# RWKV-7 recurrence followed by a squared-ReLU FFN: TensorE's work from chunk 4 on is grouped by how the array is divided, with FFN groups of two chunks

## The chip, the cores and the metric

The kernel runs on one core of one Trainium2 chip. The metric is the device time of one execution in microseconds (us). TensorE is called PE in the profile, VectorE DVE, ScalarE ACT, GpSimd POOL and SyncE SP; PEld is TensorE's weight load.

## The reference

Inputs `r, k, v, w, a, b` are float32 of 4 batches, 8 heads, 768 steps, 40 dimensions. The FFN's weights come as float64 (320 x 2048 and 2048 x 320). The output is float32, 3072 x 320.

```python
state = np.zeros((B, H, D, D))
for t in range(S):
    y[:, :, t] = np.einsum('bhd,bhde->bhe', rt, state)
    Sa = np.einsum('bhde,bhe->bhd', state, at)
    state_decay = state * wt[:, :, None, :] - np.einsum('bhd,bhe->bhde', Sa, bt)
    state = state_decay + np.einsum('bhd,bhe->bhde', vt, kt)
x = y.transpose(0, 2, 1, 3).reshape(B * S, H * D)
h = np.maximum(x @ w_in, 0.0)
out = (h * h) @ w_out
```

## The kernel before

The 768 steps are cut into 6 chunks of 128 steps for each of 4 batches. The 24 chunks (batch and place) are numbered in the order in which they run, the four batches in turn, so a chunk needs the state that the chunk four earlier left. All matmuls are float32; the trace shows each as two instructions, a transpose as one.

One chunk passes through four pieces of code, each a Python generator whose `yield` marks a place where other work may be put in between:

- `early` (called by `prepare`) turns `w`, `b`, `a` on PE, makes the running products of the decay and their reciprocals on DVE (`decay`), and makes on PE the 128 x 128 matrix N of each head (`products(bT, aT)`, L87), which goes to DRAM (`kept_d`, `kept_n`). It runs up to nine chunks ahead and ends with chunk 23 in slot 14.
- `solving` inverts the triangular halves of N on POOL (L443, L445: `half_p`, `half_t`) in units of 1 to 4 chunks and writes the inverse T to DRAM (`kept_t`). From chunk 4 on the units are chunks 4 to 5, 6 to 7, 8 to 9, 10 to 13, 14 to 17, 18 to 21 and 22 to 23. `inverses` reads T back (L459) on SP's queue.
- `rest` turns `k`, `r`, `v` and the decay on PE, makes the masked products A (k with a) and RV (v with r), decays the state, scales `k` and `b`, and turns the state (`sd`). It runs one chunk ahead.
- `chain` is the serial part: xw = v.A + state.a (L575 on); transposed (L588); times T (`times_t`, 64 x 64 quadrants); times N; times T again; transposed (L617); the new state (`grown`, from k, v and b, xn); the masked product RX; y = state.r + RV.k + RX.b. Between two steps ACT copies the result from PSUM to SBUF. y times the decay goes to `tokens`.

The main loop has a slot for each chunk i: `chain(i)`, `rest(i + 1)`, one or two `prepare`s and a share of the FFN are woven by `weave` in 12 steps by their numbers of pieces. Each engine runs its instructions in the order in which this Python code emits them.

The FFN (`ffn`, L664) works in groups of `GB = 3` chunks (384 tokens). The first layer's 320 inputs are 2 full tiles of 128 rows (`w_in`) and a rest of 64 rows (`w_third`). Two output tiles f share a step: two matmuls of 64 rows, in the array's two row halves, then four of 128 rows, then a ReLU on ACT for each (L679), then a square on DVE (L661). The second layer takes a chunk of 128 tokens at a time, 16 matmuls of 320 columns in four pieces. `by_then` sets how many pieces are done by the end of each slot: none before slot 4, 40 of 160 by the end of slot 9, 137 by the end of slot 23, the other 23 after the last slot.

PSUM is three pools of 128 x 512 banks: `ps_w` (4), `ps_c` (2, the chain's), `ps_f` (2, the FFN's). A bank is taken in turn, and its next user waits until the last reader is done.

How PE is divided follows from the operands: a matmul with 64 (or 40) rows uses half the rows (`64*128`; the profile writes `40*128`), one with a 64-wide result half the columns (`128*64`), one with both a quadrant (`64*64`), all others the whole array (`128*128`). In what follows a change of division between one PE instruction and the next is called a switch.

Of the kernel before, what the change touches and what calls it, by code (L numbers as in the profile page):

```python
# [11 lines left out]
Alu = mybir.AluOpType  # L12
# [5 lines left out]
def kernel(  # L18
# [34 lines left out]
    GB = 3  # L53
# [146 lines left out]
    hidden = single("hid", [128, NF, GB * C])  # L200
    free_words = hidden.rearrange("p f t -> p (f t)")
# [135 lines left out]
    def spare(name, i):  # L337
        at = NF * GB * C - (("mv", "turned", "joins").index(name) * 2 + i % 2 + 1) * H * Q
        return free_words[:, at:at + H * Q].rearrange("p (h t) -> p h t", h=H)

    def early(i, g=None):
# [12 lines left out]
        bT_, aT_ = turn(x_["b"]), turn(x_["a"])  # L354
        nc.vector.reciprocal(down[:, :, MID + 1:C + 1], up[:, :, MID + 1:C + 1])  # L355
        nc.vector.reciprocal(up[:, :, :MID], down[:, :, :MID])  # L356
        yield
        bT = turned("bT", 1)
# [142 lines left out]

    def rest(i, g):
        bb, c = order[i]
        x_ = loaded.pop(i)
        dec = g["dec"]
        up, down, aT = dec[:, UP], dec[:, DOWN], dec[:, A_, :, :C]
        ends = new("ends", [128, NP], 2)
        g["up"], g["aT"] = up, aT
        yield

        kT, rT = turned("kvT", 1), turned("rT", 2)
        kT_ = turn(x_["k"])
        yield
        nc.vector.tensor_tensor(kT, kT_, down[:, :, 1:C + 1], Alu.mult)  # L514
        nc.vector.tensor_copy(ends, down[:, :, 0])
        joining = inverses(i, g) if i else iter(())
        if soon(i):
            next(joining, None)
        yield
        g["A"] = masked("A", 2, kT, aT)  # L520
        yield
        while "v" not in x_:
            line.pop(0)[1]()
        nc.scalar.copy(rT, turn(x_["r"]))  # L524
        vT = turned("kvT", 1)
        nc.scalar.copy(vT, turn(x_["v"]))
        g["rT"] = rT
        yield
        if c > 0:
            st = states.tiles[bb]  # L530
            f_ = new("f", [128, NP], 1)
            nc.vector.tensor_tensor(f_, ended[bb], ends, Alu.mult)
            for e in range(2):
                own_ = st[e * DP:(e + 1) * DP, :, e, :D]
                nc.vector.tensor_tensor(own_, own_, f_[e * DP:(e + 1) * DP].unsqueeze(2).to_broadcast([DP, NP, D]), Alu.mult)
        g["RV"] = masked("RV", 4, vT, rT)
        if i and unit_of[i] < FINE:
            next(joining)
        yield
        p_ = psum(ps_w)  # L540
        for q in range(NP):
            nc.tensor.transpose(p_[:, q * 128:(q + 1) * 128], down[:, q, 1:C + 1], ident)  # L542
        inv = p_.rearrange("t (h d) -> t h d", h=H)[:, :, :D]
        yield
        for nm in ("k", "b"):
            nc.vector.tensor_tensor(x_[nm][:, :, :D], inv, x_[nm][:, :, :D], Alu.mult)
            g[nm] = x_[nm]
        g["v"] = x_["v"]
        if c > 0:
            p_ = psum(ps_c)  # L550
            for q in range(NP):
                nc.tensor.transpose(p_[:, q * 128:(q + 1) * 128], st[:, q].rearrange("p e d -> p (e d)"), ident)
            sd = g["sd"] = new("sd", [128, NP, 2, DP], 2)
            nc.scalar.copy(sd.rearrange("p q e d -> p q (e d)"), quads(p_))
        yield
        yield from joining
        yield
# [6 lines left out]
    def swap(t_, e):  # L564

        t_ = t_.rearrange("p (f t) -> p f t", f=2)
        return t_[:, ::-1] if e else t_

    def chain(i, g):
        bb, c = order[i]  # L570
        st = states.tiles[bb]
        aT, rT, k_, b_, v_ = (g[x] for x in ("aT", "rT", "k", "b", "v"))
        sd = g.get("sd")
        first, second_ = slice(0, HC), slice(HC, C)

        xw = quads(psum(ps_c))
        for h, q, e, rows in heads:
            mm(swap(xw[rows, q], 0), v_[:, h, :], swap(g["A"][e][:, q], e), h < 2)
        if c > 0:
            for h, q, e, rows in heads:  # L580
                mm(swap(xw[rows, q], 0), st[rows, q, e, :], swap(aT[rows, q], e), False)
        xc = turned("xnT", 1)
        nc.scalar.copy(xc, xw)
# [36 lines left out]
        yield  # L620
        if c < NCH - 1:
            grown = psum(ps_c)[:, :NP * D].rearrange("p (q d) -> p q d", q=NP)
            for l_, r_ in ((k_, v_), (b_, xn)):
                for h, q, e, rows in heads:
                    mm(grown[rows, q], l_[:, h, :], r_[:, h, :D], l_ is k_ and h < 2)
            for e in range(2):
                rows = slice(e * DP, (e + 1) * DP)
                nc.vector.tensor_tensor(st[rows, :, e, :D], grown[rows], st[rows, :, e, :D], Alu.add)
            ended[bb] = new(f"end{bb}", [128, NP], 1)
            nc.vector.tensor_copy(ended[bb], g["up"][:, :, C])  # L630
            yield
# [4 lines left out]
        if c > 0:  # L636
            for q in range(NP):
                mm(y_[:, q], sd[:, q].rearrange("p e d -> p (e d)"), rT[:, q], q == 0)
        for m_, rows in ((g["RV"], k_), (rx, b_)):
# [17 lines left out]
    PART = NF // 4  # L657

    def square(tiles):
        for h_ in tiles:  # L660
            nc.vector.tensor_tensor(h_, h_, h_, Alu.mult)  # L661

    def ffn():
        for gi in range(len(order) // GB):  # L664
            while gi not in gathered or finished[0] < NARROW:
                yield False
            t_ = tokens.pop(gi)
            hid = []
# [209 lines left out]
```

## Time and profile before

| | us |
|---|---|
| median of 3 runs (lowest, highest) | 1050.5 (1047.3, 1051.26) |
| profiled execution, first to last instruction | 1045.6 |
| PE busy | 927.4 (89%) |
| POOL busy | 670.6 (64%) |
| DVE busy | 496.8 (48%) |
| ACT busy | 273.0 (26%) |
| `tokens` of chunk 3, 9, 14, 23 begin at | 230.8, 470.3, 671.1, 974.4 |
| POOL writes T of chunks 10-13, 14-17, 18-21, 22-23 at | 475.1, 609.8, 747.8, 844.2 |

The profiled execution's own duration stands beside its span in no view; the median of the runs is 4.9 us above the span. Slot 4 begins at about 231 us. In the two views that matter most, the timeline has a merged row of instructions in each line (start, duration, what ran, how many), and a PE row's duration reaches past the start of the next row, as matmuls are pipelined: what a row costs is the distance between starts.

### The profile page before, as it was taken

How to read it: one execution, taken by the hardware profiler on the slowest of the kernel's cores; microseconds unless marked ns; L12 is line 12 of the kernel's file. 1: busy time of each engine (PE TensorE's matmuls, PEld its weight loads, DVE VectorE, ACT ScalarE, POOL GpSimd, SP SyncE). 2: the span in 40 equal slices, each digit the busy share in tenths (PEclk: the TensorE clock that was granted, in tenths of full speed). 3: DMA queues.
4: the chain of work that ended last, by engine and by line, in shares of the span. 5: the costliest groups of instructions: out<-in, count | busy, mean ns of one | idle time of the engine just before them, and what ended most of it. 6: DMA issues, size and time to landing. Idle time of an engine off the chain costs nothing.

```text
span 1045.6 us, 19803 instructions
## 1 busy us (share of the span) xinstructions
PE 927.4 (89%) x7824; PEld 672.1 (64%) x7824; DVE 496.8 (48%) x940; ACT 273.0 (26%) x627; POOL 670.6 (64%) x1128
## 2 busy tenths in 40 slices
PE   6364665688999999997999999999999999999998
PEld 5253455576667766775677766775677567756656
DVE  5556685796554465453744545534432432222120
ACT  3132332334332133122232132113212311232020
POOL 4778454897898599995999949999668820000000
PEclk8656676667999999998999999999999999999999
DMA  8987989688184938198564596064425432520000
GB/s 108 154 145 146 178 196 179 163 158 147 43 137 92 193 55 136 24 164 194 61 113 90 87 183 119 21 118 59 115 50 98 66 72 49 98 30 7 23 0 19
DMA packets 260360, 106.92 MB, mean 102 GB/s; under 512 B 243724, under 2 KB 249356, under 8 KB 258604
## 3 DMA queue, kind: packets, MB, share of 16 engines
q1 hardware_dynamic: 255740, 86.65, 47.8%
q0 software_dynamic: 3440, 18.88, 7.8%
q8 instruction: 62, 1.02, 0.4%
q10 hardware_dynamic: 1088, 0.13, 0.1%
q14 instruction: 30, 0.25, 0.1%
HBM read 72.47 MB, written 31.19 MB: 99 GB/s over the span
## 4 chain that ended last, share of the span: by engine, by line
PE 52%; POOL 28%; DMA 10%; issue 5%; DVE 2%; ACT 2%; SPq 1%; POOLq 0%; DVEq 0%; ACTq 0%
PE ps_f L87 26%; POOL half_t L445 14%; POOL half_p L443 13%; PE ps_w L87 11%; PE ps_c L87 10%; DMA half_n<-kept_d 3%; PE ps_w L314 2%; DMA kept_t<-half_t 1%; DMA half_n<-kept_q 1%; DMA in_w<-in_w_dram 1%; DMA T<-kept_t 1%; DMA w_out<-in_moe_w_in_dram 1%; PE ps_w L542 1%; DMA kept_m<-N 1%; POOL half_n L415 1%
## 5 line engine op out<-in xcount | busy, mean ns | idle before, releaser
L443 POOL TENSOR_TENSOR half_p<-half_n,half_t 128x70 f32<-128x70 f32 (+52 forms) x502 | 298.9, 595 | 90.2 <-DMA half_n<-kept_d 39.8
L445 POOL TENSOR_TENSOR half_t<-half_t,half_p 128x70 f32<-128x70 f32 (+52 forms) x502 | 322.4, 642 | 39.3
L87 PE MATMUL ps_f<-w_out,hid 128*128 128x320 f32 x672 | 198.6, 440 | 0.0
L87 PE MATMUL ps_f<-tokens,w_in 128*128 128x384 f32 x448 | 162.3, 506 | 0.0
L661 DVE TENSOR_TENSOR hid<-hid 128x384 f32<-128x384 f32 x128 | 94.4, 752 | 139.4 <-ACT hid L679 139.0
L87 PEld LDWEIGHTS ps_f<-w_out,hid 128*128 128x128 f32 x672 | 121.6, 190 | 44.9 <-issue 2.1
L87 PEld LDWEIGHTS ps_f<-tokens,w_in 128*128 128x128 f32 x448 | 82.1, 193 | 77.2 <-issue 33.8
L679 ACT ACTIVATE hid<-ps_f 128x384 f32<-128x384 f32 x112 | 54.9, 490 | 201.1 <-PE ps_f L87 201.1
L330 DVE TENSOR_TENSOR A<-ps_w,upper 128x512 f32<-128x512 f32 x48 | 30.9, 686 | 108.0 <-PE ps_w L87 108.0
L87 PE MATMUL ps_w<-decay,bT 40*128 40x128 f32 x352 | 31.7, 330 | 33.2 <-DVE decay L360 29.5
L514 DVE TENSOR_TENSOR kvT<-ps_w,dec 128x512 f32<-128x512 f32 x24 | 16.5, 687 | 88.7 <-DMA dec<-kept_e 46.6
L87 PE MATMUL ps_f<-tokens,w_third 64*128 64x384 f32 x224 | 55.4, 540 | 0.0
L87 PEld LDWEIGHTS ps_w<-decay,bT 40*128 40x128 f32 x352 | 26.9, 229 | 41.8 <-DVE decay L360 26.7
L87 PE MATMUL ps_c<-xr,T 64*64 64x40 f32 x768 | 39.1, 242 | 13.7 <-ACT xr L592 6.7
L351 DVE TENSOR_TENSOR_SCAN decay<-ps_w,ones 128x64 f32<-128x64 f32 x88 | 23.8, 270 | 54.2 <-PE ps_w L314 54.1
L87 PEld LDWEIGHTS ps_c<-xr,T 64*64 64x64 f32 x768 | 32.5, 148 | 25.1 <-ACT xr L592 13.1
L330 DVE TENSOR_TENSOR RX<-ps_w,upper 128x512 f32<-128x512 f32 x48 | 30.8, 683 | 26.2 <-PE ps_w L87 25.9
L330 DVE TENSOR_TENSOR RV<-ps_w,upper 128x512 f32<-128x512 f32 x48 | 30.9, 686 | 18.1 <-PE ps_w L87 17.9
L355 DVE RECIPROCAL decay<-decay 128x256 f32<-128x256 f32 x22 | 38.3, 1739 | 0.0
L356 DVE RECIPROCAL decay<-decay 128x256 f32<-128x256 f32 x22 | 37.3, 1694 | 0.0
L87 PE MATMUL ps_w<-rT,xnT 40*128 40x128 f32 x384 | 34.2, 293 | 2.4 <-ACT rT L524 2.4
L524 ACT COPY rT<-ps_w 128x512 f32<-128x512 f32 x24 | 14.0, 585 | 82.5 <-PE ps_w L314 82.5
(139 smaller groups left out, 1391.0 us busy)
## 6 DMA issues: line engine op xcount, KB each, us to landing
kept_e<-decay SPq DMA_DIRECT2D x22, 633.8 KB
dec<-kept_e SPq DMA_DIRECT2D x22, 633.8 KB
hid<-in_moe_w_out_dram SPq DMA_DIRECT2D x16, 320.0 KB
half_n<-kept_d POOLq DMA_DIRECT2D x6, 768.0 KB, 11.4
in_w<-in_w_dram SPq DMA_DIRECT2D x24, 160.0 KB
in_ab<-in_b_dram SPq DMA_DIRECT2D x24, 160.0 KB
in_ab<-in_a_dram SPq DMA_DIRECT2D x24, 160.0 KB
in_k<-in_k_dram SPq DMA_DIRECT2D x24, 160.0 KB
```

The costliest lines, as they stand in the source:

```text
L87: nc.tensor.matmul(o, l_, r_, start=start, stop=True, skip_group_check=True)
L314: nc.tensor.transpose(p_[:, q * 128:(q + 1) * 128], pair(x_, q), ident)
L330: nc.vector.tensor_tensor(t_, p_, over4(upper), Alu.mult)
L351: nc.vector.tensor_tensor_scan(up[:, q, MID + 1:C + 1], wT[:, q, MID:], ones, 1.0, Alu.mult, Alu.mult)
L355: nc.vector.reciprocal(down[:, :, MID + 1:C + 1], up[:, :, MID + 1:C + 1])
L356: nc.vector.reciprocal(up[:, :, :MID], down[:, :, :MID])
L443: nc.gpsimd.tensor_tensor(p_, part[:, at:at + m_].unsqueeze(1).to_broadcast([128, n, m_]), t3[:, :n, s:s + 1].to_broadcast([128, n, m_]), ...
L445: nc.gpsimd.tensor_tensor(t3[:, :n, s + 1:], t3[:, :n, s + 1:], p_, Alu.subtract)
L514: nc.vector.tensor_tensor(kT, kT_, down[:, :, 1:C + 1], Alu.mult)
L524: nc.scalar.copy(rT, turn(x_["r"]))
L661: nc.vector.tensor_tensor(h_, h_, h_, Alu.mult)
L679: nc.scalar.activation(h_, p_, Act.Relu)
```

## The change

Slots 0 to 3 stay woven (`woven`), without FFN work, which they did not have before either. From slot 4 on each slot is written out by hand (`sorted_slot`): the pieces of chain, rest, prepare and FFN stand in a fixed order in which pieces with one division of the array follow each other. The first matmuls of a chain (v.A) move to the end of the slot before, behind the other 128*64 work. `rest` is cut into functions (`turn_k`, `make_a`, `turn_rv`, `decay_state`, `make_rv`, `turn_down`, `scale_kb`, `turn_state`) with the same instructions. In `early` the turning of `b` and `a` moves behind the reciprocals, a piece of its own (`apart`).

The FFN works in groups of 2 chunks (256 tokens). A step makes four output tiles ("a quad") in two banks: `thirds` issues the four 64-row matmuls, `whole` the eight 128-row ones, then two ReLUs and two squares of 128 x 512. A ring of 6 quads holds the hidden layer. Second-layer work comes in quarters of a chunk (`make_quarter`: 4 tiles, 8 instructions). A slot has two quads and four quarters; slot 4 has two more quads; what is left runs in `Ffn.rest` after slot 23.

The product of state and a is one 128 x 128 block-diagonal matmul for a pair of heads in place of two in quadrants. The copy of xw is three copies, the upper half's column halves exchanged there, not in the matmul's operands. `grown` is a 128-row, 128-wide matmul of 80 columns for a pair of heads in place of two 64-wide ones of 40 columns; the blocks off the diagonal are not read. The POOL work, `solving`, the units and the slots of the prepares are as before; the loads of the next chunk are issued at fixed places (`k`, the decay and `b` at the slot's start, `r` and `v` a slot earlier). `spares` gets memory of its own; two of its three tiles have one buffer in place of two.

```diff
-    GB = 3
+    GB = 2
...
-    hidden = single("hid", [128, NF, GB * C])
+    hidden = single("hid", [128, QUADS, 2, 2 * GB * C])
...
         xw = quads(psum(ps_c))
         for h, q, e, rows in heads:
-            mm(swap(xw[rows, q], 0), v_[:, h, :], swap(g["A"][e][:, q], e), h < 2)
+            mm(xw[rows, q], g["v"][:, h, :], g["A"][e][:, q], h < 2)
+        yield
         if c > 0:
-            for h, q, e, rows in heads:
-                mm(swap(xw[rows, q], 0), st[rows, q, e, :], swap(aT[rows, q], e), False)
+            for q in range(NP):
+                mm(xw[:, q], st[:, q].rearrange("p e d -> p (e d)"), g["aT"][:, q], False)
         xc = turned("xnT", 1)
-        nc.scalar.copy(xc, xw)
+        nc.scalar.copy(xc[low], xw[low])
+        for n in range(2):
+            nc.scalar.copy(xc[high, :, n * HC:(n + 1) * HC], xw[high, :, (1 - n) * HC:(2 - n) * HC])
...
             for l_, r_ in ((k_, v_), (b_, xn)):
-                for h, q, e, rows in heads:
-                    mm(grown[rows, q], l_[:, h, :], r_[:, h, :D], l_ is k_ and h < 2)
+                for q in range(NP):
+                    mm(grown[:, q].rearrange("p (e d) -> p e d", e=2), pair(l_, q), r_[:, 2 * q:2 * q + 2, :D], l_ is k_ and q == 0)
...
+        def thirds(self):
...
+            self.banks = [psum(ps_w if self.tail else ps_f).rearrange("p (f t) -> p f t", f=2) for _ in range(2)]
+            for n in range(2):
+                for e, p_ in enumerate(self.banks):
                     half = slice(e * DP, (e + 1) * DP)
+                    at = ((k % NQ) * 2 + n) * 128
+                    mm(p_[:, n], w_third[half, at:at + 128], t_[half, NT, :], n == 0)
+
+        def whole(self):
...
+            for e, p_ in enumerate(self.banks):
+                for n in range(2):
+                    f = (k % NQ) * QF + 2 * n + e
                     for j in range(NT):
+                        mm(p_[:, n], w_in[:, j, f * 128:(f + 1) * 128], t_[:, j, :], False)
+                h_ = hidden[:, self.place(k), e]
+                nc.scalar.activation(h_, p_.rearrange("p f t -> p (f t)"), Act.Relu)
...
+        loads()
+        step(on(ch), halves)
+        if more:
+            begin(j, n)
+        step(of(turn_rv), on(one), second.make_quarter, on(one), halves)
+        step(on(ch), halves)
+        if early_join:
+            next(joining, None)
+        fetch_next(j + 1, "r")
+        step(second.make_quarter, halves)
+        extra()
+        step(on(ch))
+        step(of(make_rv), second.thirds)
+        step(on(ch), on(one), on(two), on(two))
+        if fine:
+            next(joining, None)
+        step(second.whole, on(two))
+        step(on(ch))
+        step(on(one), of(turn_k))
+        step(on(ch), of(decay_state), on(one), of(turn_down), of(scale_kb))
+        step(on(ch), of(turn_state), second.square)
+        if fine:
+            next(joining, None)
+        step(on(ch), of(make_a), second.thirds, on(one))
+        fetch_next(j + 1, "v")
+        step(second.whole, on(two), on(two))
+        if not early_join:
+            next(joining, None)
+        step(on(ch), extra)
+        step(on(ch))
+        if more:
+            later_chain = n["chain"] = chain(j, n)
+            next(later_chain)
+        run(ch)
+        step(second.square, second.make_quarter)
+        step(second.make_quarter, on(two))
```

Here `ch` is the chain of the slot's chunk i, `of` a piece of `rest` for chunk j = i + 1, `one` and `two` the prepares, `joining` the load of T for j; `early_join` is true where j lies in the unit of i, and `extra` makes a quad in slot 4 alone.

## The prediction

> **What bounds the kernel now.** I read the page's busy shares first, then the busy time slot by slot, the chain of waits around the one hole in PE's work, and PE's timeline of one slot.
>
> ```profile
> PE 927.4 (89%) x7824; PEld 672.1 (64%) x7824; DVE 496.8 (48%) x940; ACT 273.0 (26%) x627; POOL 670.6 (64%) x1128
> ...
> PE   6364665688999999997999999999999999999998
> ...
> POOL 4778454897898599995999949999668820000000
> ```
>
> After some 230 us PE is busy in nearly every slice, POOL until about 845 us. By slot (length, PE busy, PEld, DVE, ACT, POOL busy, PE's granted clock, DMA share, GB/s):
>
> ```profile
> 435.00:471.00 36.00, 35.49 (x338) 27.62 (x337) 17.50 (x41) 9.19 (x22) 32.94 (x40) 1.00 0.78 135
> 471.00:519.00 48.00, 42.32 (x337) 28.81 (x336) 23.90 (x39) 11.87 (x27) 34.72 (x54) 0.93 0.69 133
> 519.00:558.00 39.00, 38.68 (x329) 27.54 (x328) 22.41 (x38) 9.91 (x23) 36.57 (x32) 1.00 0.51 87
> 779.00:811.00 32.00, 31.46 (x287) 23.12 (x285) 7.87 (x17) 6.80 (x16) 28.61 (x44) 1.00 0.44 85
> ```
>
> Slots 9, 11 and 18 are PE's; DVE and ACT are far below. Slot 10 has a hole, and the chain of waits says whose it is:
>
> ```profile
> 475.06 4.75 DMA kept_t<-half_t
> ...
> 480.52 8.87 DMA T<-kept_t
> ...
> 489.53 1.08 PE ps_c L87 x16
> ```
>
> POOL finishes the inverse of chunks 10 to 13 at 475.06; written and read back, it reaches PE at 489.5. So two clocks run: PE's work, and POOL's (475.06, 609.8, 747.8, 844.2 us, solves back to back). Before slot 10 they are level; afterwards PE is late by itself. Now one slot of PE (start, duration, what, count; a row's cost is the distance to the next start):
>
> ```profile
> 778.54 2.32 PE L87 MATMUL ps_f<-w_out,hid 128*128 128x320 f32 x8
> 780.69 0.60 PE L552 MATMUL ps_c<-ident,state 128*128 128x128 f32 x4
> 781.13 2.32 PE L87 MATMUL ps_f<-w_out,hid 128*128 128x320 f32 x8
> 783.38 1.09 PE L87 MATMUL ps_c<-A,in_v 128*64 128x128 f32 x16
> 784.40 1.10 PE L87 MATMUL ps_c<-dec,state 64*64 64x128 f32 x16
> 785.43 2.42 PE L87 MATMUL ps_f<-w_out,hid 128*128 128x320 f32 x8
> 787.69 0.60 PE L588 MATMUL ps_c<-ident,xnT 128*128 128x128 f32 x4
> 788.83 0.66 PE L87 MATMUL ps_c<-xr,T 64*64 64x40 f32 x16 [0.54 <-ACT xr L592]
> 789.42 2.42 PE L87 MATMUL ps_f<-w_out,hid 128*128 128x320 f32 x8
> 791.77 0.66 PE L87 MATMUL ps_c<-minus_x,N 64*64 64x40 f32 x16
> ```
>
> The same eight second-layer instructions cost 2.15 us with no switch beside them (778.54), 2.25 with one behind (781.13), 2.26 with one ahead (785.43), 2.35 between two (789.42). **A switch costs 0.20 us** beside 128-wide weights; beside 64-wide weights and transposes (0.44 alone, 0.50 with one, 0.59 between two) it is 0.15.
>
> **PE's clock before 489.5 us.** A slot after the change, with a prepare, without switches: ten transposes of four 4.4; N, A, RV and RX 0.90 each (798.71 to 802.89 us in the timeline, switches taken off), 3.6; v.A and state.a 0.88 each; RV.k and RX.b 1.8; state.r 0.9; T, N, T 1.4; `grown` 1.75 (below); two quads 8.6; four quarters 8.6: 32.8. Its order has ten switches, 1.8 us; with the waits below it is 37.5. Slot 4 has two quads more and two quarters less (+4.3), slot 5 a second prepare (+4), so six slots from 231 us end near 464, and the first product with T is due at 471. T comes at 489.5, as POOL's code and order do not change. What slots 4 to 9 save becomes a wait of some 18 us for T (5.4 now). So the sum is made from 489.5 to the end at 1045.6, 556.1 us; the FFN stands the same at that point in both, 72 of 96 quarters left.
>
> **The change part by part, from 489.5 us on.**
>
> *Switches.* I counted them in the list of PE's instructions: 284 up to the end of slot 23, 16 after it; 300 at 0.18 on the mean is 54 us. The written order has ten in each of 14 slots (into and out of the three quadrant steps, two 64*128 groups, one 128*64 group) and two in each of six quads at the end: 152, mostly 0.15 to 0.20, 26.6 us. Saved: **27**. If the drain alone (0.095) went it would be 14, if all were at 0.20, 30.
>
> *First layer.* Left before: 47 pairs (376 `w_in` instructions of 384 columns at 0.322, 188 `w_third`), 3.23 us each without switches; after: 34 quads of 16 instructions of 256 columns, 0.215 each by the same price per column, and 0.87 for the eight `w_third`: 4.32. 152 against 147: **-5**. It is a little more work done before 489.5, not cheaper work. A 256-column matmul is not in the trace; 0.842 ns per column holds for 320 columns (2.156 / 8) and 384 alike. ReLU and squares are as many elements in fewer instructions, on engines that have room.
>
> The Trainium skill speaks against this part: its page "TensorE: Matmul & The Clock Gate" (Part 3, "The mechanism") says that a weight load overlaps running matmuls only when it goes to another row group. By that rule 168 more full-array `w_in` loads at its 107 ns (LDWEIGHTS: columns / 1.2) would be an estimated 18 us more, and the time 1048. The trace disagrees: the eight instructions at 778.54 follow each other at 0.269, which is their 320 columns and no load, though all take the whole array.
>
> *State products.* state.a: eight instructions of 128 columns at 0.11 (state.r, 0.89) for 0.88: nothing. `grown`: the two blocks of 16 take 1.07 us now (799.80 to 800.87), 0.92 without switches. After: 16 instructions of 80 columns with 128-wide weights. No row has that. By columns they cost 0.067 each, by the nearest row, transposes and state.r with the same weights, 0.109. I take 0.109, as that row's matmuls are no longer than the loads they need: 1.75 us, +0.83 in ten slots, **+8** (lower end +1.5). The three copies of xw are 0.29 to 0.6 us more on ACT; r, v, w and a quarter (3.5 us of PE) lie between them and the transpose.
>
> *Moved.* r and v of chunk 11 are turned before 489.5: **-1**. v.A moves past its chain's copies of `sd`; its inputs are ready. The loads of k, decay and b are issued at slot start and used 15 us in; decay took 6.4 us from issue to use (684.6 to 691.1), so they are hidden, and the 8 us of cover would be lost only if SP stood behind T.
>
> *Waits that go.* PE's rows since 489.5 priced without waits are 482 us, with switches 536; the last matmul ends 552.8 after 489.5, so **16** are waits. 4.7 are the quadrant steps behind ACT's xr (788.83), where a quarter now stands; others are N and RX behind ACT and DVE, 1.7 the lower clock after the hole.
>
> *Waits that come.* In slots with a prepare, N comes last in the second 64*128 group and takes the PSUM banks of RX (four banks in turn). RX's masks stand on DVE behind kT, ends, f, two state scalings, bT, decay, k, b, two adds, one copy and two squares: by their rows 0.6+0.2+0.4+0.9+0.6+0.6+0.4+0.4+0.65+0.2 and two squares of 512 columns (0.56 to 1.0 for 384), 1.5 to 2.7, then 1.25. That is 7.7 to 8.9 us after k is turned (15.9 us into the slot), against PE's arrival at N at 21.9. PE waits 1.7 to 2.9 us, some of it already at RX; behind it wait `whole`, state.r and the rest of the chain, so it all counts. I take the upper end, as POOL is busy in these slots and the slow squares are those beside POOL: 2.9 in slots 10 to 14, 14.5. Without a prepare only the second transposition (xn) has short cover, 0.44 us of k for a round trip over ACT of about 1: 0.5 in nine slots, 4.5. The lower clock after the hole, 1.7, stays. **+21.** If the cover held everywhere it is 2; with a whole uncovered round trip in each of the 14 slots, 30.
>
> *Sum:* 556.1 - 27 - 5 + 8 - 1 - 16 + 21 = 536, so the span ends at 1025.6; the median stands 4.9 above the span: **1030 us**. Slot 14 then asks for its T at about 642, slot 18 at 777, and POOL's come at 624 and 762 (14.3 after the solve, as at 475.06): no second hole.
>
> **The rivals.** *No wait on DVE:* the squares run at 0.75 and RX's masks come in time. Then 1030 - 15 = 1015; POOL's T for slot 18 (762) is then just due, so less than 1010 is not to be had however PE gains. For it: DVE is busy only 24 of 48 us in slot 10. Against: its queue is in order.
>
> *Half the price:* the first load after a switch stays exposed for another cause, and only the drain goes: +13, 1043. Against: 785.43 shows the load's part plainly.
>
> *Slower:* the fixed order makes the chain's round trips PE-ACT-PE waits. There are six in a slot (xc, xr, xn, xr, xn, xT), with one block as cover where `weave` spread the FFN over twelve steps. The row at 788.83 shows the price, 0.54 behind a cover of 0.44, and ACT is in order: a ReLU of 512 columns, some 0.62 by the row of 384 (0.49), may stand ahead. Two trips a slot at 1.2 are 2.4 in 14 slots, 34: 1064. It decides from 1.5 us a slot (20 / 14). Against: the covers are 3.5, 2.2, 1.9, 3.6, 0.4 to 1.3 and 2.6 us.
>
> That a quad is skipped since its ring place is taken is a rival too: by my count 42 quads and 78 quarters are done by slot 23, none skipped; a skipped one moves behind the last slot and uncovers the step it stood behind, as in the slower case.
>
> **Chances.** Forecast (1022 to 1038) 0.48; no wait on DVE (1008 to 1022) 0.17; half the price, or as much in small waits (1038 to 1052) 0.18; slower 0.17. T's arrival may shift all by 5 either way (its two transfers took 13.6 us; slots 0 and 1, which set POOL's start, change little). A measurement here tells 0.5%, 5 us, from no change. Faster by more: 0.48 + 0.17 + two thirds of 0.18 = 0.77; within it 0.08; slower 0.15. The range leaves out the slower case and the lowest few us: 1008 to 1054.
>
> **What would show it.** PE idle of 15 to 20 us before the first product with T in slot 10, at 485 to 495; ten switches a slot after it; quarters at 2.15; `grown` at 0.11 an instruction; in slots 10 to 14 2 to 3 us before N or RX put down to DVE; slots 15 to 19 at about 33 us. It is wrong if T of slot 10 does not bind (slots 4 to 9 over 42 us each), or if waits on ACT exceed 1.5 us a slot.

## The result and the profile after

The changed kernel takes 1087.9 us (median of 4 runs, 1076.6 to 1095.0) against 1049.4 (1047.3 to 1051.3): a ratio of 1.034, 95% interval 1.029 to 1.040. The forecast was 1030. The ratios and intervals here and below leave out runs more than 1.5% above the fastest of their kernel, as the profiled ones here and of x9 are; the medians keep them. The profiled execution is thus the longest of the four, with a span of 1093.2, so its trace shows the loss at its largest; the four spans go with the mean granted clock: 1074.9 at 0.887, 1086.1 at 0.881, 1086.4 at 0.876, 1093.2 at 0.870. Before it was 1045.6 at 0.915. Even the shortest is 29 us longer than that.

From the page of the changed kernel, PE's busy share, then PE, POOL and the granted clock in 40 slices:

```profile
PE 952.3 (87%) x7728; PEld 785.3 (72%) x7728; DVE 491.6 (45%) x908; ACT 284.4 (26%) x643; POOL 669.4 (61%) x1128
...
PE   6275765685899899999899999999999999999998
...
POOL 4788544886885399993699976999768810000000
PEclk8666575566998898999988998989999999999999
```

The clock's row of the kernel before:

```profile
PEclk8656676667999999998999999999999999999999
```

PE issues 96 instructions fewer than before (7824) and is busy 25 us longer. The clock's rows show what it meets: after the start (ten slices, 273 us) the clock is down to 0.8 in a slice again and again, up to about 740 us, where the kernel before has a 9 in all slices but one. Slots 4, 10, 14 and 17 of the changed kernel, from tokens to tokens (length, PE busy, PEld, DVE, ACT, POOL, granted clock, DMA share, GB/s):

```profile
239.59:304.70 65.11, 48.68 (x448) 40.70 (x450) 31.94 (x63) 21.63 (x48) 52.56 (x106) 0.81 0.48 87
515.71:565.73 50.02, 43.88 (x332) 35.28 (x330) 18.59 (x33) 11.69 (x27) 37.00 (x51) 0.86 0.75 136
688.33:730.31 41.98, 40.19 (x316) 33.30 (x314) 20.97 (x33) 10.10 (x23) 39.24 (x36) 0.88 0.38 73
796.00:828.50 32.50, 32.39 (x284) 26.70 (x282) 11.68 (x21) 8.42 (x19) 23.97 (x48) 1.00 0.35 66
```

Slot 17 has the forecast's length (about 33). Slot 14 has 1.8 us without PE, yet PE is busy 40 us for work that was priced at 34.6: the clock is 0.88 on the mean. PE's timeline shows where it falls, at the end of slot 13 (three rows) and in slot 14 (two):

```profile
674.20 1.03 PE L87 MATMUL ps_f<-tokens,w_third 64*128 64x256 f32 x7
676.80 2.60 PE L87 MATMUL ps_w<-decay,bT 40*128 40x128 f32 x16 [1.58 <-DVE RX L332]
679.33 6.18 PE L87 MATMUL ps_f<-tokens,w_in 128*128 128x256 f32 x16
...
711.03 1.06 PE L87 MATMUL ps_c<-minus_x,in_b 128*128 128x80 f32 x8
713.38 0.63 PE L561 MATMUL ps_c<-ident,state 128*128 128x128 f32 x4 [1.29 <-DVE state L536]
```

N (`ps_w<-decay,bT`) waits 1.58 us for a bank that the masks of RX hold. Then N takes 2.53 us, start to start, where 0.9 to 1.1 is usual, and `whole` 6.01 where 3.65 is. In the clock's records of this trace 677.51 to 684.34 is at half speed. In slot 14 the state's transposes (L561) wait 1.29 us for its decay on DVE (L536), and 715.06 to 725.30 is at half speed. PE's waits from slot 4 to the end, in sum, times, longest:

```profile
PE ps_c L561 <- DVE state L536: 11.9, 12, 1.7
PE ps_w L87 <- DVE RX L332: 9.9, 8, 3.5
PE ps_w L545 <- DMA dec<-kept_e: 7.1, 2, 4.5
PE ps_f L87 <- DVE w_out L266: 6.3, 1, 6.3
```

T is not among them. An account of all the time after slot 3 follows from each trace: idle is time in which no matmul runs; clock is half of the time in which PE works at half clock; work is the rest, the busy time as it would be at full clock.

| us | before | after | difference |
|---|---|---|---|
| until tokens of chunk 3 | 230.8 | 239.6 | +8.8 |
| idle | 25.6 | 51.3 | +25.7 |
| clock | 10.1 | 49.5 | +39.4 |
| work | 779.0 | 752.8 | -26.2 |
| span | 1045.6 | 1093.2 | +47.6 |

**The saving is there, 26 us of it, and in this execution it is lost 2.5 times over to waits and to the clock behind them.**

### The profile page after: what moved, and what is told of

Its sections match the earlier page's. It is cut to its first block, busy times and chain, and to the rows that moved or that the text cites. A ratio compares the mean times of both kernels' runs of the same rounds, so it can differ in the third digit from the quotient of the medians.

```text
span 1093.2 us, 19699 instructions
## 1 busy us (share of the span) xinstructions
PE 952.3 (87%) x7728; PEld 785.3 (72%) x7728; DVE 491.6 (45%) x908; ACT 284.4 (26%) x643; POOL 669.4 (61%) x1128
## 4 chain that ended last, share of the span: by engine, by line
PE 66%; DVE 12%; DMA 8%; issue 4%; ACT 4%; POOL 3%; SPq 2%; ACTq 0%; DVEq 0%; POOLq 0%
PE ps_f L87 36%; PE ps_c L87 13%; PE ps_w L87 11%; PE ps_w L316 4%; DMA in_w<-in_w_dram 2%; DMA dec<-kept_e 2%; DVE hid L742 1%; SPq L108 1%; DVE state L536 1%; PE ps_c L621 1%; POOL half_t L450 1%; POOL half_p L448 1%; DVE RX L332 1%; DMA blocks<-kept_t 1%; DVE kvT L510 1%
## 5 line engine op out<-in xcount | busy, mean ns | idle before, releaser
L450 POOL TENSOR_TENSOR half_t<-half_t,half_p 128x70 f32<-128x70 f32 (+52 forms) x502 | 323.4, 644 | 39.3
L87 PE MATMUL ps_f<-w_out,hid 128*128 128x320 f32 x768 | 221.0, 438 | 0.0
L87 PEld LDWEIGHTS ps_f<-w_out,hid 128*128 128x128 f32 x768 | 142.0, 191 | 54.9 <-issue 4.4
L87 PE MATMUL ps_f<-tokens,w_in 128*128 128x256 f32 x672 | 172.7, 415 | 0.0
L87 PEld LDWEIGHTS ps_f<-tokens,w_in 128*128 128x128 f32 x672 | 136.2, 208 | 27.0 <-issue 5.6
L742 DVE TENSOR_TENSOR hid<-hid 128x512 f32<-128x512 f32 x96 | 83.4, 904 | 64.7 <-ACT hid L735 64.7
L735 ACT ACTIVATE hid<-ps_f 128x512 f32<-128x512 f32 x84 | 50.2, 597 | 142.5 <-PE ps_f L87 142.5
L683 DVE TENSOR_TENSOR tokens<-ps_c,dec 128x512 f32<-128x512 f32 x24 | 16.6, 690 | 133.5 <-PE ps_c L87 133.5
L87 PE MATMUL ps_f<-tokens,w_third 64*128 64x256 f32 x336 | 54.0, 427 | 6.3 <-DVE w_out L266 6.3
L614 ACT COPY xnT<-ps_c 64x512 f32<-64x512 f32 x24 | 13.9, 579 | 145.7 <-PE ps_c L87 145.6
L87 PEld LDWEIGHTS ps_f<-tokens,w_third 64*128 64x128 f32 x336 | 37.1, 214 | 9.2 <-DVE w_out L266 6.6
L87 PE MATMUL ps_w<-dec,kvT 40*128 40x128 f32 x384 | 38.6, 335 | 1.1 <-DVE in_b L551 0.9
```

What stands on the lines that cost most here:

```text
L87: nc.tensor.matmul(o, l_, r_, start=start, stop=True, skip_group_check=True)
L450: nc.gpsimd.tensor_tensor(t3[:, :n, s + 1:], t3[:, :n, s + 1:], p_, Alu.subtract)
L683: nc.vector.tensor_tensor(t_, y_, g["up"][:, :, :C], Alu.mult)
L735: nc.scalar.activation(h_, p_.rearrange("p f t -> p (f t)"), Act.Relu)
```

## The experiments

Two theories stood at first. A: the waits that the written order brings make PE idle, and idle time also brings half clock. B: the clock falls for another reason (PE's work in part of the array, the new form of the products). Ratios are to the kernel before, which took 1048.0, 1048.6, 1049.7 and 1048.7 us (medians) beside the four groups of runs.

**x1, squares and N later.** The squares go behind the masks of RX and A on DVE, N behind the second `whole` on PE.

```diff
-        step(on(ch), of(turn_state), second.square)
+        step(on(ch), of(turn_state))
...
-        step(on(ch), of(make_a), second.thirds, on(one))
+        step(on(ch), of(make_a), second.thirds, second.square)
...
-        step(second.whole, on(two), on(two))
+        step(second.whole, on(one), on(two), on(two))
```

> The changed kernel with two things moved in the slots from 4 on: the squares go behind the masks of RX and A on DVE, and the products N go behind the second `whole` on PE. The same instructions otherwise, two more switches a slot (0.4 us). Theory A (a wait of 1 to 3 us at N brings the granted clock to half for the next 3.4 to 13.7 us, and that costs more than the wait): without the wait the half-clock stretches between 300 and 730 us go, slots 5 to 14 take 36 to 37 us in place of 39 to 46, the time comes to 1030 to 1050. Theory B (the clock falls because of the 64-row work itself, whatever waits): the clock stays at 0.85 to 0.9 in these slots, only the wait of 1.5 to 2 us goes, slots at 39 to 40, time 1065 to 1075.

Measured 1065.0 us, ratio 1.017 (1.013 to 1.021). After slot 3 idle is 38.4 and clock 31.7. Of the 31 us that these two terms lose between the two traces (12.9 and 17.8), more than half is clock and not waiting; the medians differ by less, 22.9 us. The time is the lower end of B's (1065), and slots 5 to 14 have B's length, 39.7 us on the mean; their clock, 0.94, is above B's (0.85 to 0.9). The state's transposes still wait, 3.8 us in slots 11 to 14. This run alone does not part A and B.

**x2, more work in front of the wait.** The first pair of the second `thirds` of a slot is issued four times more in slots with a prepare: idle becomes busy, and nothing else is moved.

```diff
-            for n in range(2):
+            for n in [0] * fill + [0, 1]:
...
-        step(on(ch), of(make_a), second.thirds, on(one))
+        step(on(ch), of(make_a), lambda: second.thirds(4 if made else 0), on(one))
```

> The changed kernel with PE work added: in slots with a prepare the first pair of the second `thirds` is issued four more times (16 instructions of 256 columns in two row halves, 1.7 us; the last one overwrites the others, so the result is the same). PE then works where it waited for N's banks; all orders and waits stay. Theory A (half clock after idle time): the clock goes up to 0.97 or more in slots 5 to 14 and a slot gets 1 to 3 us shorter although 1.7 us of work is added; time 1050 to 1070. Theory B (the clock falls for another reason than idle time): clock as before, slots the same or up to 2 us longer; time 1085 to 1110.

Measured 1086.9 us, ratio 1.037 (1.032 to 1.042): 15 us more work (768.1 against 752.8), 31 us less at half clock (79.2 against 110.2), and the time of the changed kernel. That is B's time (1085 to 1110), not A's (1050 to 1070). But B left the clock as it was, and it rises. Slots 5 to 14 together (length, PE busy, granted clock, DMA share, GB/s), of the changed kernel and of x2:

```profile
304.78:730.31 425.53, 398.74 (x3212) 0.90 0.56 104
```

```profile
307.18:722.35 415.17, 394.33 (x3372) 0.94 0.58 107
```

Over whole executions it is 0.885 to 0.892, against 0.870 to 0.887. Work that is not needed paid for itself through the clock: A's direction, at less than A's size.

**x3, the kernel before with the block-diagonal state products alone** (`grown`, state.a and the three copies of xw, as in the change).

> The kernel before with the state products of the changed one alone (state.a and grown as block-diagonal 128-wide matmuls, xw copied in three pieces). By PE's rows grown costs 0.8 us more, and a switch (0.15) goes with state.a: +0.6 us in each of 16 slots from 4 to 19, +10 us if PE bounds all, +6 to 7 if the wait for T of slot 10 takes those of slots 4 to 9. If the three copies of xw lengthen the chain where it has no cover (a transpose follows at once in some slots), up to 0.5 us a slot more, +15 to 18.

Measured 1066.5 us, ratio 1.019 (1.014 to 1.024). Work after slot 3 is 789.2 against 779.0: **+10**, some 0.6 us in each of the 16 slots that have `grown`. The rest is start (+2.9) and clock (+5.4) in single slots. The time, 18.5 us up, is the upper forecast's (+15 to 18), but not for its reason: idle time is 25.2 us, against 25.6. This part of the change costs by itself; it has no half clock of its own in slots 7 to 14, which speaks against the half of B that blames the form of the products.

**x4, every known wait moved.** x1, and the state's decay (with the copy of its `ends`) goes from behind a later chain step to behind the first `whole`, and the additional quads of slot 4 go behind that too.

```diff
-        step(second.whole, on(two))
+        step(second.whole, on(two), of(make_ends), of(decay_state))
+        extra()
...
-        step(on(ch), of(decay_state), on(one), of(turn_down), of(scale_kb))
+        step(on(ch), on(one), of(turn_down), of(scale_kb))
```

> x1 and two more moves: the state is decayed right behind the first `whole` (before k is turned), and in slot 4 the additional quad is made behind the first `whole` instead of ahead of the first product with T, where it waited 6.3 us for a PSUM bank that the rounding of the weights held. Theory A: the waits on the state (0.4 to 1.7 us in 12 slots) and their half-clock time go as well; slots 5 to 14 at 35 to 36 us, slot 4 under 55; T of chunks 10 to 13 becomes due and PE waits for it; time 1020 to 1035, below the kernel before. Theory B: as x1 less 0.5 to 1 us a slot, 1055 to 1065.

Measured 1042.9 us, ratio 0.995 (0.993 to 0.998). The same instructions as after, and 45 us less. Slots 11 to 14 together (length, PE busy, granted clock, DMA share, GB/s), of the kernel before:

```profile
518.90:671.10 152.20, 150.93 (x1293) 1.00 0.57 104
```

of the changed kernel:

```profile
565.73:730.31 164.58, 156.68 (x1252) 0.91 0.52 97
```

and of x4:

```profile
540.33:679.56 139.23, 139.23 (x1253) 1.00 0.61 115
```

In x4 PE is never idle in these slots and never at half clock: 34.8 us a slot, where the forecast's prices without waits gave 34.6. The same work in parts of the array is there at full clock, so it does not bring the clock down. B falls. A's time (1020 to 1035) is missed by 8 us: slot 4 takes 61.2 us and not under 55, with a wait of 7.5 for r, and T of slot 10 is waited for, 6.1 us.

**x8, x9, x10: the price of one wait.** x8 is x4 with the squares and N where the change has them. x9 and x10 add one and three idle operations of 128x256 on DVE ahead of the masks in slots with a prepare.

```diff
+        for _ in range(1 if made else 0):
+            nc.vector.tensor_tensor(filler, filler, filler, Alu.mult)
```

> The kernel x4_all_moved with one thing put back as the change has it: the squares ahead of the masks of RX and A on VectorE, and N ahead of the second set of whole first-layer tiles on TensorE. TensorE then waits for a bank that the masks of RX hold, once a slot in the slots that make an early chunk (up to 14), by 1.4 to 1.6 us each in the changed kernel. Nothing else of the slot is touched, so it prices one wait. Theory A (the wait also brings 3.4 to 6.8 us of half clock): slots 11 to 14 go from 34.8 to 38 to 41 each, half clock in the rows of each, slots 15 to 22 as before at 32.5 and 30.8; time about 1060. Rival B (a wait costs its own length): 36.3 each, no half clock, time about 1050.

> The kernel x8_n_early (N waits once a slot for a bank that the masks of RX hold, about 0.9 us, slots 11 to 14 at 35.9, 35.6, 35.0 and 36.3, none of them at half clock) with one more idle operation on VectorE ahead of those masks in the slots that make an early chunk: 128x256, some 0.5 us by the 0.96 us of a square of 128x512, so a wait of about 1.4 us. What the runs so far suggest: the clock is granted in windows of 3.41 us on a fixed grid, and a window in which TensorE was busy for less than about two thirds is followed by one to four at half speed. Theory A (that rule): a wait of 1.4 us is over a third of a window if it falls in one and not if it is cut by the grid's line, so about half of the slots 5 to 14 show 3.4 to 6.8 us of half clock; slots 11 to 14 between 36 and 40, mean 38. Rival B (idle time costs its own length at any dose; the half clock comes from something else): 36.2 each, no half clock.

> As the run with one idle operation, but with three of them: a wait of some 2.4 us. Theory A (windows of 3.41 us, less than two thirds busy, the next at half): a wait of 2.4 us leaves a window under two thirds wherever it falls but for a cut near its middle, so nearly every slot from 5 to 14 shows half clock; slots 11 to 14 from 39 to 43, that is 34.8 and 2.4 of waiting and 2 to 5 more. Rival B (length alone): 37.2 each, no half clock.

Measured 1062.1 us (ratio 1.012, 1.009 to 1.016), 1085.4 (1.029, 1.023 to 1.036) and 1108.7 (1.055, 1.051 to 1.059). Slots 11 to 14 of x8 in the same columns:

```profile
550.69:693.42 142.73, 140.37 (x1252) 1.00 0.60 112
```

of x9, and below it PE's wait in them (sum, times, longest):

```profile
571.39:728.40 157.01, 150.57 (x1252) 0.93 0.56 102
```

```profile
PE ps_w L87 <- DVE RX L332: 6.0, 4, 2.0
```

and the same two of x10:

```profile
581.02:748.29 167.27, 151.34 (x1253) 0.91 0.51 96
```

```profile
PE ps_w L87 <- DVE RX L332: 15.9, 4, 5.0
```

| slots 11 to 14, us | idle | at half clock | clock's cost | length over x4 |
|---|---|---|---|---|
| x8 | 2.4 | 0 | 0 | 3.5 |
| x9 | 6.4 | 20.5 | 10.2 | 17.8 |
| x10 | 15.9 | 30.7 | 11.9 | 28.0 |
| after | 7.9 | 30.7 | 14.9 | 25.4 |

In x8's trace idle time of 0.6 us a slot cost 0.9 in these slots, as B said, and A's 38 to 41 us a slot did not come there; of the 12 us that this trace has over x4's, 10 lie ahead of slot 11, with 71.7 us at half clock against 51.2. But the trace is of the shortest of nine executions (1053.0), and the median has the time that A gave (about 1060). Waits of 1.6 us cost 4.4, waits of 4 us (2.4 were expected) 7.0: both inside what A gave for x9 (36 to 40 a slot; 39.3, in its longest execution) and x10 (39 to 43; 41.8). Over all of slots 4 to 14 the masks of RX hold PE up by 5.4, 13.9 and 36.1 us in the three traces, and the medians are 19, 42 and 66 us above x4's: by an estimate from these, a wait cost 1.8 to 3.5 times its length.

How much of a wait it takes, the clock's records show. In each of the 16 traces the clock changes only on a grid of 3.413 us (no change is off by more than a thousandth of a step). I cut the time after slot 3 along it. Of windows at full clock in which PE was busy under 55%, 73 of 77 were followed by one at half clock; of 55 to 65%, 30 of 43; 65 to 70%, 8 of 21; 70 to 75%, 2 of 18; above, 6 of 3332. A window at half clock was followed by another in all 63 cases with PE busy under 75%, in half of the others (124 of 248). So a wait of over about 1.2 us (35% of 3.413) that falls into one window mostly brings windows at half clock, one to four in 107 of 119 stretches and up to eight in the others; one that the grid cuts in two may bring none. The grid lies differently in each execution, which may be why the same kernel's time scatters; that is not shown.

The Trainium skill's page "TensorE: Matmul & The Clock Gate" (Part 1, "What's actually happening") has this window, 3413 ns and free-running, and the traces agree. It puts the fall to half clock after a whole idle window, and its rule ("HAM oscillation") is to have no gaps over about 3.4 us; by that, the 1.58 us above would have cost nothing more. The traces differ: half a window is enough.

**x5, r and v of chunk 5 ahead of the token moves.** On SP they stood behind eight moves and came 7.5 us late in slot 4.

```diff
+            jobs.append(((fetch_next(i + 2, nm) for nm in ("r", "v")), 2, 10, 11))
...
-                fetch_next(i + 2, "r", "v")
```

> This is the kernel of the run before (squares, N, the state's decay and the odd first-layer group all moved behind the waits) with one more edit: r and v of chunk 5 are fetched at the end of slot 3 ahead of the eight token moves on SP, and not behind them. There slot 4 took 61.2 us, with 7.5 us in which r's transposes wait for the transfer and half clock behind it. Theory A (idle time costs the clock too): slot 4 loses the 7.5 us of waiting and some 6 us of half clock, 61 -> 47; slot 5 ends near 326 instead of 340, GpSimd's unit of chunks 10 to 13 starts earlier by as much, and T of slot 10, which bound it there by 6 us, comes near 498: all slots after it move by 13, to a time of about 1030 us. Rival B (the wait alone, the clock is low in slot 4 for another reason): slot 4 loses 7 us, the time is 1036. Rival C (GpSimd binds slot 10 whatever slot 4 does, by another input): T of slot 10 stays at 511.6 and the time stays at 1042.

Measured 1036.4 us, ratio 0.989 (0.984 to 0.993). The wait for r is gone; slot 4 goes from 61.2 to 55.8, not to 47, as 4.9 us before the first third tiles (a bank of the rounding) and 13.7 at half clock stay. T of slot 10 still binds there, 5.6 us, but POOL's solve ends at 486.0 and not at 497.0 (4.2 us of that is an earlier start of slot 4), so it is not C. The time is B's 1036 and not A's 1030, yet half clock in slot 4 goes from 23.9 us to 13.7, as A had it: A's direction at half its size.

**x6, the first slots' pieces back:** k turned a step earlier, the chain's first piece undivided in slots 0 to 3.

> The kernel of the run x5 with the pieces of the first four slots put back as they were before the change: k is turned one step earlier, the chain's first products and its state products are one piece again in slots 0 to 3 and do not run ahead (from chunk 4 on nothing differs). The changed kernel and every version with its slots 0 to 3 begin slot 4 some 9 us later than the kernel before; the version of the kernel before that has the block-diagonal products alone does not. Theory A (the split of the pieces costs those 9 us): tokens of chunk 3 begin near 231 instead of 240, all that follows moves by 9, GpSimd's units too: a time 7 to 9 us under x5, about 1021. Rival B (the single buffers that the inverses of the first chunks share, which stay): 240 and the time of x5.

Measured 1037.8 us, ratio 0.990 (0.986 to 0.993): x5's time, tokens of chunk 3 at 237.7 against 237.6. A falls.

**x7, `grown` in quadrants of columns again** (x6 with the kernel before's 32 instructions).

> The kernel of the run x6 with the products that add to the state made in quadrants again (16 of 64 columns of the array into 64 partitions per pass of k and b, as in the kernel before), the rest block-diagonal. In the run with the block-diagonal products alone each slot from 7 on was longer by 0.7 us. Theory A (the doubled output of grown is what costs): 0.7 to 0.8 us less in each of the slots 4 to 22, less two more switches of the array's division at 0.15 to 0.20 us each: slots 15 to 19 at 32.1 instead of 32.5 and a time some 7 us under x6. Rival B (the three copies on ScalarE or the products with the state cost the 0.7 us): slots as in x6 or 0.3 us longer, no gain.

Measured 1032.0 us, ratio 0.983 (0.980 to 0.986). Slots 15 to 19 are 32.0 (32.5 in x6), work after slot 3 is 740.0 us against 747.6. The time gains 5.8 us (some 7 were said). The doubled product costs, as A said.

**x12, two switches more.** The second `thirds` of a slot, four products of 64 rows, leaves the masks' group and stands between two groups of transposes.

```diff
-        step(on(ch), on(one), of(turn_down), of(scale_kb))
+        step(on(ch), second.thirds, on(one), of(turn_down), of(scale_kb))
...
-        step(on(ch), of(make_a), second.thirds, second.square)
+        step(on(ch), of(make_a), second.square)
```

> The kernel x7_grown_quadrants with the second set of third-tile products of a slot (four products of 64 rows, 0.96 us) moved from behind the masks of A, which have 64 rows too, to between two groups of transposes of the whole array. The same instructions, two switches of the array's division more in each of the slots 5 to 23. Theory A (a switch costs 0.15 to 0.20 us, as taken in the prediction): slots 15 to 19, which wait for nothing, go from 32.0 to 32.3 or 32.4, some 7 us in all. Rival B (a switch costs nothing by itself, and what the change saved came from larger products): 32.0 each and the time of x7. Rival C (moving the products earlier or later brings a wait): slots differ from each other and the profile shows PE waiting for a bank of theirs.

Slots 15 to 19 are 32.36 us each against 32.01 in x7: 0.35 for two switches, with no wait in them. PE's timeline in slot 19 of x7:

```profile
819.66 0.66 PE L658 MATMUL ps_c<-ident,minus_x 128*128 128x128 f32 x4
820.15 0.60 PE L551 MATMUL ps_w<-ident,dec 128*128 128x128 f32 x4
...
824.22 1.03 PE L87 MATMUL ps_f<-tokens,w_third 64*128 64x256 f32 x8
825.18 3.72 PE L87 MATMUL ps_f<-tokens,w_in 128*128 128x256 f32 x16
```

and of x12:

```profile
821.92 0.66 PE L658 MATMUL ps_c<-ident,minus_x 128*128 128x128 f32 x4
822.51 1.14 PE L87 MATMUL ps_f<-tokens,w_third 64*128 64x256 f32 x8
823.57 0.66 PE L551 MATMUL ps_w<-ident,dec 128*128 128x128 f32 x4
```

The transposes of minus_x cost 0.49 with the next group like them, 0.59 with `thirds` behind; `thirds` cost 0.96 in the masks' group and 1.06 between two switches. A's price holds. The time does not show it: 1029.8 us, ratio 0.980 (0.978 to 0.983), no slower than x7, as slots 4 to 10 came out 5 us shorter (idle 20.6 and clock 18.6, against 25.7 and 21.9). What the waits up to slot 10 scatter is as much as these switches cost.

**x11 and x13, the start.** x11 is x7 with two buffers again for the first inverses' scratch tiles; x13 is x11 with the first group's token moves at the end of slot 2, where groups of three have theirs.

> The kernel x7_grown_quadrants with the two scratch tiles of the first inverses (mv and turned, one buffer each since the change) in two buffers again for chunks 1 and 3, in a part of the hidden activations that is not yet used then. Theory A (the single buffers make the first slots longer, as putting the pieces back did not shorten them): tokens of chunk 3 begin some 5 to 9 us before the 233.7 of x7, and GpSimd's T of slot 10 comes earlier by as much; a time of 1024 to 1027. Rival B (the first slots hang on transfers and on GpSimd's inverses, and what differs is where these fall): no shift beyond 3 us, a time within 3 us of x7.

> The kernel x11_spares_apart with the eight token moves of the first group of two chunks issued on SP at the end of slot 2 (where the kernel before, with groups of three, has its first ones) and not at the end of slot 1. Its slots 0 to 2 then differ from the kernel before in nothing but their FFN tiles' place. Theory A (the moves of about 7 us on SP, ahead of the loads of slot 2, make slot 2 longer): slot 2 goes from 57.6 to about 51, tokens of chunk 3 begin near 233, and the time comes to 1026. Rival B (the start differs by scatter of the transfers from run to run, as 233.7 and 238.1 in two runs with the same first slots suggest): tokens of chunk 3 between 233 and 240 again, slot 2 within 3 us of 57, time within 3 us of 1031.

x11: 1031.5 us, ratio 0.983 (0.981 to 0.986), tokens of chunk 3 at 239.3, later than in x7 by more than B's 3 us: no gain, A falls. x13: 1030.7 us, ratio 0.982 (0.979 to 0.985). Its slot 2 takes 49.9 us (57.6 in x11) and tokens of chunk 3 begin at 231.6, the kernel before's 230.8: there A holds, and x14, with the same first slots, has 50.2. So part of the longer start came from eight moves on SP ahead of slot 2's loads. One profile is shown of each, and two with the same first slots (x7 and x12) differ by 4.4 us, so its size is uncertain. The time did not follow: at tokens of chunk 10 only 3.1 of the 7.7 us are left.

**x14, rounding earlier:** x13 with two pairs of rounding steps more in slot 3 (`3: (9, TOTAL)` for 7).

> The kernel x13_moves_later with two more pairs of rounding steps of w_out done in slot 3 and so out of slot 4, where the first third-tile products wait 4.8 us for a bank that the rounding holds on VectorE. Theory A (that wait and the half clock behind it make slot 4 longer): the wait goes, slot 4 is shorter by 5 to 10 us with 3 to 7 us less at half clock, slot 3 longer by at most 3; T of slot 10 then binds by some 5 us more, so that the time gains 0 to 5 us. Rival B (VectorE is the bound of slots 3 and 4, the rounding's cost only moves): slot 3 longer by what slot 4 gains, no gain.

1033.5 us, ratio 0.986 (0.984 to 0.989). The wait for the rounding's bank (4.6 us in x13) is gone, and the one for a ReLU's bank grows from 3.5 to 5.5; slot 4 takes 60.5 (60.7), slot 3 44.6 (42.0). Rival B. Why slot 4 is so long in every version stays open in its detail; it holds two quads more than other slots.

x7, x11, x12 and x13 are the fastest, 2% below the kernel before, and not told apart. Their 1030 to 1032 us are the forecast's number by other kernels than the one forecast, and do not bear it out.

## Why the prediction was wrong, point by point

The span was forecast at 1025.6 and came out at 1093.2 in the trace, 67.6 more. The first product with T in slot 10 comes at 533.4 and not at 489.5: 43.9 us of the miss. From there to the end it is 559.8 us and not 536: the other 23.7. Apart from a start that was 8.8 us later, both parts are mostly short waits of PE and the half clock behind them. **Two steps failed: "Waits that come", for which the clock's price was left out, and the cover of 18 us before T of slot 10, under which any delay in slots 4 to 9 was priced at nothing.**

- **Switches: right.** 0.15 to 0.20 us each and ten a slot; x12 measured 0.175. Quarters are 2.16, slots 15 to 19 32.5 to 33.1 (about 33 was said).
- **First layer and state products: right.** Sixteen `w_in` instructions take 3.56 to 3.65 (3.44 by the price per column, and its switch), the loads stay hidden. `grown` measured 0.107 an instruction (0.109 taken); x3 puts the whole of that part at 10 us in 16 slots, 0.6 each (0.83 taken).
- **The sum of work: right.** From the first product with T in slot 10 to the end, work is 518.3 us against 543.3 before, -25; the terms gave -27 - 5 + 8 - 1 = -25.
- **Waits that go: too large.** 16 us were taken to go after 489.5; there the kernel before is idle 10.9 us and loses 1.9 to the clock, 12.7 in all.
- **Waits that come: failed, by its price.** N behind RX's masks was named rightly, with place and engine. It was oversized: in slots 11 to 14 it is 3.8 us in four, against 2.9 each. The idle time of slots 11 to 23 is 12.6 us, under the 16 taken for them (11.6 and 4.5). What was not priced is the clock behind it: 16.6 us in slots 11 to 23, 49.5 in all after slot 3. From the first product with T in slot 10 on, 19.8 us of idle time and 21.7 of clock stand against the 21 of the sum. "The lower clock after the hole" stood in the sum as 1.7, for one hole of the kernel before; I took it for that hole's and not as the price of every wait. A wait not named cost 11.9 us in 12 pieces: the state's transposes behind its decay on DVE, which the order puts right in front of them (L536, L561).
- **Slots 4 to 9 at 37.5 us, ending near 464: failed.** They end at 515.7, 46.0 us each on the mean: the prediction's own sign of being wrong, over 42. 8.8 is the start ("slots 0 and 1 change little"); the rest stands in 29.2 us of idle time and 26.1 of clock in slots 4 to 9, where 17 were allowed for waits (2.9 in each). The loads of dec, taken as hidden, were waited for 7.1 us in two; r behind the token moves on SP and the rounding's banks were not looked for, because I counted on a cover of 18 us. That cover was too wide by itself: the product with T comes 12 us into a slot (688.3 to 700.55), not 7, as 464 and 471 have it.
- **T of slot 10 pins POOL's clock: failed.** PE never waits for T. That POOL's code and order do not change does not hold its times: its solves wait for N, which PE makes, 40.6 us in three waits against 7.3 in one before (the lines below). One of them, 13.8 us up to 359.5, stands ahead of the solve of chunks 10 to 13, which is done at 498.3 and not at 475.1. PE late makes POOL late. In x4 and x5 T does bind, by 6 us.
- **The rivals.** The slower case was PE-ACT-PE round trips; ACT is in none of the larger waits. Another mechanism made it slower. No quad is skipped: each slot from 5 on has its 32 `w_in` instructions. Priced by the runs (between 4.4 for 1.6 us and 7.0 for 4), the 2.9 us that I had in hand behind RX's masks would be an estimated 5.8 in each of slots 10 to 14, 29 and not 14.5, and as much again in slots 5 to 9, which I let vanish in the cover of 18 us: on the slower side.

POOL's waits for N in the changed kernel, in sum, times, longest, and the one ahead of the solve of chunks 10 to 13:

```profile
POOL half_n L420 <- DMA kept_d<-N: 40.6, 3, 14.7
```

```profile
359.53 1.03 POOL L420 DMA_DIRECT2D half_n<-kept_d  x2 [13.78 <-DMA kept_d<-N]
```

## What to carry to other kernels

Price a wait of the bounding engine with what follows it: in this kernel the waits of x8, x9 and x10 cost an estimated 1.8 to 3.5 times their length, and instructions that save half a microsecond a slot are soon outweighed. When an order is written out by hand, look for each product's last reader or writer on the other in-order queues (DVE's masks, the state's decay, SP's loads behind stores) and put those first: the moves of x4 alone made 45 us of difference with the same instructions. A date of another engine is no fixed point when that engine reads what the delayed one makes.

## What the runs showed of the hardware that was not expected

The clock falls to half by windows of 3.413 us on a grid that runs through, mostly when PE works less than about two thirds of one window; it comes back on the same grid, mostly after one to four windows. Work that nobody reads, put into idle time, gave back as much as it cost (x2). Eight 320-column products follow each other at 0.269 us with a full-array load each, and a 128-row, 128-wide product of 80 columns takes 0.107 us, more than its columns (0.067).
